# The spectral middle of a GFNet block on the 64-row halves of the matmul array

## The chip, the cores and the metric

The kernel runs on one core of one Trainium2 chip. The core has a matmul engine (PE, with its weight loads listed as PEld), three elementwise engines (DVE, ACT, POOL) and DMA queues, which are fed here by SP and by POOL. The metric is the device time of one execution in microseconds (us); lower is better.

## What is computed

A pre-norm transformer block on 2048 tokens of width 576 in bfloat16: a two-dimensional Fourier filter as the mixer, and a GeGLU feed-forward network.

```python
def _A_ref(x, w_r, w_i):
    B, S, D = x.shape
    X = rfft2(x.astype(float32), axes=(-2, -1))
    X = X * (w_r + 1j * w_i)                  # w: [2048, 289]
    return irfft2(X, s=(S, D), axes=(-2, -1)).astype(bfloat16)

def _B_ref(x, w_gate, w_up, w_down):          # [576, 4608] twice, [4608, 576]
    return (gelu(x @ w_gate) * (x @ w_up)) @ w_down

h = x + _A_ref(layernorm(x), w_r, w_i)
h2 = h + _B_ref(layernorm(h), w_gate, w_up, w_down)
```

## The kernel before

Every instruction is written out by hand. `Prog` keeps, for each tile's key, the last writer and the readers, and turns them into semaphore waits; each engine runs its own list strictly in the order in which it was filled. PE does not wait for its own earlier matmuls, except where an operation names them (`after`). The order of the stages is written as strings of short words: `SEQ1` for stage A, `SEQF` for the spectral middle, `SEQ` for the inverse stage. A letter is a step, the number says which piece, and a table beside it (`DENG`, `BENG`, `VENG`) says which engine evicts it from PSUM.

**Stage A** (`a_mm`, L532). The 2048 tokens are 128 partitions times 16 tiles c. One matmul per tile, column block and half of D does the first part of the token transform, with tables `ATS` scaled by the layer norm's 1/sigma, into `U`. Five column blocks k: 1 and 3 are differences and need the negated second half of x (`XN[...,0:288]`, made by `x_neg`, L548, step n, on POOL), 0 and 2 are sums, 4 is the remainder of 32 + 32 columns (`x_tail`, L553, step t, on POOL, copies one of them beside the other). Tiles go through in six groups; for groups 2, 3 and 4 POOL also scales the tables (`ln1_scale`, L501, step x); M0 to M5 are the groups' matmuls. The evictions into `U` (`a_ev`, L543) are shared by ACT and DVE.

**The spectral middle** works on 16 pieces i, one residue g each (`GORD` is 1 to 15, then 0). For every piece:

- D (`st_D`, L609): the real transform over the 576 columns, 2 outputs (odd and even) of 3 matmuls each, 128x288, into a pair of PSUM banks; evicted to `CUS` (576 elements a partition).
- B (`st_B`, L619): the last part of the token transform, 4 matmuls of 128x288 with 128-row tables `BT`; evicted to `YS`.
- T (`st_T`, L628): the product with the filter on DVE, Y times (w_r, -w_i, w_i, w_r): 1152 products a partition from `YS` and `WS` into `TP`. `WS` holds three planes, the third of which DVE makes as the negated w_i (`st_w`, L633, step w).
- Z (`st_Z`, L639 and L642): DVE adds the products in pairs, the 256 main columns into `ZS`, the last 32 into `ZR`, four pieces side by side.
- V (`st_V`, L649): back over the tokens, 4 matmuls of 128x256, one PSUM bank, evicted to `V` by ACT.
- R (`st_R`, L661 and L664): the same for the 32 remaining columns of four pieces at once, 2 matmuls; DVE multiplies the result by a mask `MK` into `VR`.

**After it**: I and N (L726, L764), the inverse transform over columns and the last part over tokens, which adds to x in `XO`. Eight token tiles (`NPRE`) are done here; the other eight are put between the matmuls of the first quarter's `down` (`def_i`, `def_n`, with tiles `EB`, `QB`, `YB`, `JD`). Then the feed-forward network in four quarters of 512 tokens: `gu_part` (L848) does gate and up; since 576 is 4.5 times 128 it runs on the 64-row halves of the array, two matmuls side by side on partitions 0 to 63 and 64 to 127 with different banks, each half in a first and a second part; `down` (L935) follows.

**DMA.** SP's queue issues, one after the other: x and the A tables, FT, BT, the filter's first half (residues 0 to 8, w_i then w_r, five loads each), VT, the second half (six each), DT, IT, DP, ITD, IDT, and the up weights. POOL's queue issues the gate weights: slot 0 waits for the filter's second half, slots 1 and 2 lie where `WS` is and wait for the last T. SBUF is full, so most tiles share their place with later ones; `P.alias` passes the waits on.

Of the kernel before, what the change touches and what calls it, by code (L numbers as in the profile page):

```python
# [4 lines left out]
BF16 = mybir.dt.bfloat16  # L5
# [39 lines left out]
def build_tables():  # L45
# [26 lines left out]
    I = I.reshape(4, 16, 2, 16, 128).transpose(1, 0, 2, 3, 4)  # L72
# [63 lines left out]
    T["BTAB"] = B.reshape(2, 3, 128, 128).transpose(2, 0, 1, 3).reshape(128, -1)  # L136
    T["VTAB"] = V.reshape(2, 2, 128, 256).transpose(2, 0, 1, 3).reshape(128, -1)
# [175 lines left out]
def _build(nc, A_x, A_w_r, A_w_i, B_w_gate, B_w_up, B_w_down, out):  # L313
# [16 lines left out]
    WS = sb.alloc("WS", [128, 3, NG, K2], BF16)  # L330
    assert sb.off <= wgu_end
    sb.off = wgu_end
    V = sb.alloc("V", [128, NT, 4, NG, 8], BF16)
    VR = sb.alloc("VR", [128, NT, 2, NG, 8], BF16)
# [8 lines left out]
    sb.off = wgu_end  # L343
    EB = sb.alloc("EB", [128, 2 * HK], F32)
    QB = sb.alloc("QB", [128, 4, HK], F32)
    YB = sb.alloc("YB", [128, D], BF16)
    JD = sb.alloc("JD", [128, D], BF16)
    assert sb.off <= wgu_end + NPRE * 4 * NG * 8 * 2
# [19 lines left out]
    U = sb.alloc("U", [128, 5, NG, NT, 8], BF16)  # L368
# [8 lines left out]
    BT = sb.alloc("BT", [128, 2, 3, 128], BF16)  # L377
    VT = sb.alloc("VT", [128, 2, 2, 256], BF16)
    end1 = sb.off
    sb.off = h_off  # L380
    HT0 = sb.alloc("HT0", [128, 5, 512], BF16)

# [8 lines left out]
    YS = sb.alloc("YS", [128, 2, 2, KW], BF16)  # L391
    TP = sb.alloc("TP", [128, 2, 2, 2, KW], BF16)
    ZS = sb.alloc("ZS", [128, NZ, 2, 256], BF16)
    ZR = sb.alloc("ZR", [128, 2, 2, 128], BF16)
# [38 lines left out]
    def w_up(pl, hf):  # L433
        g0, g1 = ((0, 9), (9, 16))[hf]
        src = (A_w_r, A_w_i)[pl].tensor
        P.dma(SP, WS[0:64, 1 + pl, g0:g1, :].rearrange("p g k -> p (g k)"), bass.AP(src, g0 * K2, [[128 * K2, 16], [16 * K2, 4], [1, (g1 - g0) * K2]]),
              f"w{pl}{hf}", w=[("W", hf, pl, 0)])

    def w_down(pl, hf):
        g0, g1 = ((1, 9), (9, 16))[hf]  # L440
        src = (A_w_r, A_w_i)[pl].tensor
        for jj in range(4):
            P.dma(SP, WS[64 + jj:128:4, 1 + pl, g0:g1, :], bass.AP(src, (64 + 16 * jj + 16 - g0) * K2, [[128 * K2, 16], [-K2, g1 - g0], [1, K2]]),
                  f"w{pl}{hf}", w=[("W", hf, pl, 1 + jj)])
        if hf:
            P.dma(SP, WS[64:128, 1 + pl, 0, :], bass.AP(src, 64 * K2, [[128 * K2, 16], [16 * K2, 4], [1, K2]]), f"w{pl}{hf}", w=[("W", hf, pl, 5)])

# [8 lines left out]
    wkeys = [[("W", hf, pl, h) for pl in range(2) for h in range(5 + hf)] for hf in range(2)]  # L456
# [62 lines left out]
    def a_mm(i):  # L519
        c0, c1 = GROUPS[i]  # L520
        for k in AORD:
            b = a_bank(i, k)
            for c in range(c0, c1):
# [7 lines left out]
                for lhs, p0, p1, s, e in parts:  # L531
                    P.op(PE, lambda t, b=b, lhs=lhs, p0=p0, p1=p1, s=s, e=e, o=o, c=c: t.matmul(bank(b, p0, p1, o, o + 128), lhs, ATS[:, c, :], start=s, stop=e),  # L532
                         r=[("X", c), ("ATS", c)] + ([("XN", c)] if k % 2 or k == 4 else []) + ([("XT", c), "XZ"] if k == 4 else []), w=[("PS", b)])

    def a_ev(n, eng, late=False):
        i, k = n // 5, AORD[n % 5]
        hs = (1,) if late else (0,) if n in SPLIT else (0, 1)
        g0, g1 = 8 * hs[0], 8 * hs[-1] + 8
        c0, c1 = GROUPS[i]
        m, b, w = c1 - c0, a_bank(i, k), 128  # L540
        src = bank(b, 0, w, 0, 128 * m).rearrange("p (n g e) -> p n g e", n=m, g=16)[:, :, g0:g1, :]
# [4 lines left out]
    def x_neg(i):  # L546
        c0, c1 = GROUPS[i]
        P.op(POOL, lambda g: g.tensor_scalar(XN[:, c0:c1, 0:288], XO[:, c0:c1, 288:D], -1.0, 1.0, op0=ALU.mult, op1=ALU.mult),  # L548
             r=[("X", c) for c in range(c0, c1)], w=[("XN", c) for c in range(c0, c1)])

    def x_tail(i):
        c0, c1 = GROUPS[i]
        P.op(POOL, lambda g: g.tensor_scalar(XN[:, c0:c1, 288:320], XO[:, c0:c1, 256:288], 1.0, 1.0, op0=ALU.mult, op1=ALU.mult),  # L553
             r=[("X", c) for c in range(c0, c1)], w=[("XT", c) for c in range(c0, c1)])

    P.op(DVE, lambda v: v.memset(XN[:, :, 320:384], 0.0), w=["XZ"])
# [18 lines left out]
    P.alias([(k, c) for k in ("XN", "XT") for c in range(NT)], [("V", g, c) for g in range(NG) for c in range(2)])  # L575
# [4 lines left out]
    FB, used = {}, [0] * 8  # L580
    for t, w in enumerate(SEQF):
        k, i = w[0], w[1:].rstrip("abc")
        if k in "DB":
            late = ("V", 0) in FB or any(x[0] == "V" for x in SEQF[t:t + 4])
            b = min((0, 2, 4) if late else (0, 2, 4, 6), key=lambda b: max(used[b], used[b + 1]))
            used[b] = used[b + 1] = t + 1
        elif k in "VR":
            b = min((6, 7) if ("D", LAST) not in FB else range(8), key=lambda b: used[b])
            used[b] = t + 1
            if k == "V":  # L590
                b2 = b
                if int(i) == LAST and len(VENG[LAST]) > 1:
                    b2 = min(range(8), key=lambda b: used[b])
                    used[b2] = t + 1
                b = (b, b2)
        else:
            continue
        FB[k, int(i)] = b
# [5 lines left out]
    def st_D(i, eng=ACT):  # L604
        b0, s3 = FB["D", i], i % 3
        for o in range(2):
            b = b0 + o
            for m, us in enumerate((1 - o, 3 - o, 4) if o == 0 else (4, 1 - o, 3 - o)):
                P.op(PE, lambda t, b=b, m=m, us=us, o=o: t.matmul(bank(b, 0, 128, 0, 2 * HK), U[:, us, i, :, :], FT[:, 3 * o + (2 if us == 4 else us // 2), :], start=(m == 0), stop=(m == 2)),  # L609
                    r=[("U", q, us, i // 8) for q in range(len(GROUPS))] + ["FT"], w=[("PS", b)])  # L610
        ev(eng, CUS[:, s3, :, :].rearrange("p a (j r) -> p a j r", r=2), banks(b0, 2, 2 * HK).rearrange("p r (a j) -> p a j r", a=2),
           [("PS", b0), ("PS", b0 + 1)], [("CU", s3)])

    def st_B(i, eng=ACT):
        sl, s3, sp_ = i % 2, i % 3, 1 if GORD[i] == 0 else 0
        b0 = FB["B", i]
# [387 lines left out]
```

## Time and profile before

Three runs of the kernel took 491.55, 491.62 and 493.1 us; the median is 491.62. The profiled execution has a span of 489.7 us.

| | us | share of the span | instructions |
|---|---|---|---|
| span of the profiled execution | 489.7 | | 9878 |
| PE busy | 481.8 | 98% | 4357 |
| PEld (weight loads) | 290.9 | 59% | 4358 |
| DVE busy | 191.3 | 39% | 384 |
| ACT busy | 152.0 | 31% | 294 |
| POOL busy | 32.6 | 7% | 65 |
| L848, gate and up | 228.5 + 53.4 | 58% | 2142 + 486 |
| L935, down | 144.3 | 29% | 1152 |
| L609, D | 13.4 | 3% | 96 |
| L619, B | 9.7 | 2% | 64 |
| L628, T | 12.1 | 2% | 17 |

Shares of busy time are means over stages with different limits. PE's 98% is mostly the feed-forward network; in the spectral part DVE and ACT are full as well. The busy time of a group is the time in which at least one of its instructions ran. A mean duration is longer than the distance between two in a row, because an engine starts the next one before the last has left its pipeline. The granted clock is 1.00 in all stretches looked at.

### The profile page before, as it was taken

What the parts mean: (1) busy time and instruction counts of PE and PEld (TensorE: products, weight loads), DVE (VectorE), ACT (ScalarE), POOL (GpSimd) and SP (SyncE); (2) the same over time, 40 slices, a digit from 0 to 9 for tenths busy, and PEclk for the clock granted to TensorE, in tenths of its full rate; (3) what the DMA queues carried; (4) which work ended last, traced back from release to release, by engine and by line L of the source; (5) the groups of instructions that cost most, each with busy time, mean ns of one, the idle gap of its engine ahead of it and who ended that gap; (6) DMA issues with size and microseconds to landing.
All of it is one profiled execution on the core that took longest, in us unless ns stands there. A gap on an engine that the chain in (4) does not pass through costs nothing.

```text
span 489.7 us, 9878 instructions
## 1 busy us (share of the span) xinstructions
PE 481.8 (98%) x4357; PEld 290.9 (59%) x4358; DVE 191.3 (39%) x384; ACT 152.0 (31%) x294; POOL 32.6 (7%) x65
## 2 busy tenths in 40 slices
PE   6999999999999999999999999999999999999998
PEld 3887865555688744444577644444677544444775
DVE  7899823443455534333311144333211233333111
ACT  6999852232322223322200033233100122323000
POOL 5411541000000020000000000000000000000000
DMA  8990998111000071100000001000000000000000
GB/s 282 231 335 11 367 358 304 62 26 24 1 18 14 13 230 26 23 4 1 0 20 19 14 17 26 14 1 1 7 19 19 6 1 1 1 1 1 14 18 19
DMA packets 25147, 31.26 MB, mean 64 GB/s; under 512 B 11440, under 2 KB 17840, under 8 KB 25104
## 3 DMA queue, kind: packets, MB, share of 16 engines
q1 hardware_dynamic: 22208, 18.68, 13.4%
q0 software_dynamic: 2896, 11.95, 7.0%
q8 instruction: 34, 0.56, 0.5%
q14 instruction: 9, 0.07, 0.1%
HBM read 26.29 MB, written 2.36 MB: 58 GB/s over the span
## 4 chain that ended last, share of the span: by engine, by line
PE 93%; ACT 3%; DMA 2%; DVE 2%; SPq 1%; issue 0%; DVEq 0%
PE PS L848 57%; PE PS L935 29%; DMA XO<-in_A_x_dram 2%; PE PS L609 2%; PE PS L726 1%; DVE TP L628 1%; ACT V L601 1%; PE PS L886 1%; PE PS L764 1%; PE PS L619 1%; PE PS L532 1%; ACT U L543 1%; ACT YS L601 1%; SPq L223 1%; PE PS L900 0%
## 5 line engine op out<-in xcount | busy, mean ns | idle before, releaser
L848 PE MATMUL PS<-HT,WG 64*128 64x512 bf16 (+1 forms) x2142 | 228.5, 372 | 0.0
L848 PEld LDWEIGHTS PS<-HT,WG 64*128 64x128 bf16 x2142 | 109.4, 94 | 117.5 <-issue 0.7
L857 DVE TENSOR_TENSOR AT<-GL,PS 128x512 bf16<-128x512 bf16 x144 | 98.8, 687 | 177.5 <-ACT GL L856 177.5
L856 ACT ACTIVATE GL<-PS 128x512 bf16<-128x512 f32 x144 | 85.9, 597 | 262.1 <-PE PS L848 248.7
L935 PE MATMUL PS<-WD,AT 128*128 128x288 bf16 (+2 forms) x1152 | 144.3, 286 | 0.0
L935 PEld LDWEIGHTS PS<-WD,AT 128*128 128x128 bf16 x1152 | 110.8, 98 | 30.7 <-ACT GL L856 1.3
L938 DVE TENSOR_TENSOR OS<-PS,XO 128x288 bf16<-128x288 f32 (+2 forms) x32 | 14.6, 457 | 100.4 <-PE PS L935 100.4
L848 PE MATMUL PS<-HT,WGX 64*128 64x512 bf16 x486 | 53.4, 376 | 0.0
L848 PEld LDWEIGHTS PS<-HT,WGX 64*128 64x128 bf16 x486 | 23.7, 94 | 28.8
L755 ACT ACTIVATE JD<-XO,NM 128x576 bf16<-128x576 bf16 x8 | 6.2, 775 | 28.4 <-DVE XO L903 28.4
L609 PE MATMUL PS<-FT,U 128*128 128x288 bf16 x96 | 13.4, 286 | 0.0
L628 DVE TENSOR_TENSOR TP<-YS,WS 128x1152 bf16<-128x1152 bf16 (+2 forms) x17 | 12.1, 720 | 2.1 <-ACT YS L601 1.6
L532 PE MATMUL PS<-ATS,XO 128*128 128x128 bf16 x96 | 8.8, 219 | 3.4 <-POOL ATS L501 2.4
L475 DVE BATCH_NORM_STATS2 ST<-XO 128x6 f32<-128x288 bf16 x26 | 10.0, 442 | 2.3 <-DMA XO<-in_A_x_dram 2.2
L609 PEld LDWEIGHTS PS<-FT,U 128*128 128x128 bf16 x96 | 9.2, 98 | 2.4
L601 ACT ACTIVATE CUS<-PS 128x576 bf16<-128x576 f32 x16 | 10.2, 658 | 0.8 <-PE PS L609 0.4
L601 ACT ACTIVATE YS<-PS 128x576 bf16<-128x576 f32 x16 | 10.0, 654 | 0.7 <-DVE TP L628 0.7
L619 PE MATMUL PS<-CUS,BT 128*128 128x288 bf16 x64 | 9.7, 286 | 0.3 <-ACT CUS L601 0.3
L543 ACT ACTIVATE U<-PS 128x384 bf16<-128x384 f32 (+2 forms) x28 | 9.6, 414 | 0.9 <-PE PS L532 0.9
L532 PEld LDWEIGHTS PS<-ATS,XO 128*128 128x128 bf16 x96 | 6.8, 98 | 5.0 <-POOL ATS L501 3.0
L903 DVE TENSOR_TENSOR XO<-PS,XO 128x576 bf16<-128x576 f32 x8 | 6.1, 757 | 8.0 <-PE PS L900 8.0
L601 ACT ACTIVATE V<-PS 128x512 bf16<-128x512 f32 (+1 forms) x17 | 8.9, 588 | 0.0
(79 smaller groups left out, 206.0 us busy)
## 6 DMA issues: line engine op xcount, KB each, us to landing
WD<-in_B_w_down_dram POOLq DMA_DIRECT2D x9, 576.0 KB, 12.0
WG<-in_B_w_up_dram SPq DMA_DIRECT2D x4, 1152.0 KB, 7.7
WG<-in_B_w_gate_dram POOLq DMA_DIRECT2D x4, 1152.0 KB, 10.1
out_dram<-OS SPq DMA_DIRECT2D x30, 72.0 KB, 1.6
XO<-in_A_x_dram SPq DMA_DIRECT2D x3, 576.0 KB, 7.2
WGX<-in_B_w_up_dram SPq DMA_DIRECT2D x1, 1152.0 KB, 5.9
WGX<-in_B_w_gate_dram POOLq DMA_DIRECT2D x1, 1152.0 KB, 9.7
HT<-HN SPq DMA_TRANSPOSE x60, 2.4
```

The source lines that it names most:

```text
L475: P.op(DVE, lambda v: v.bn_stats(ST1[:, c, h, :], XO[:, c, 288 * h:288 * h + 288]), r=[("X", c)], w=[("ST1", c, h)])
L532: P.op(PE, lambda t, b=b, lhs=lhs, p0=p0, p1=p1, s=s, e=e, o=o, c=c: t.matmul(bank(b, p0, p1, o, o + 128), lhs, ATS[:, c, :], start=s, sto ...
L543: fn = (lambda v: v.tensor_copy(dst, src)) if eng == DVE else (lambda a: a.activation(dst, src, ACTF.Copy))
L601: fn = (lambda v: v.tensor_copy(dst, src)) if eng == DVE else (lambda a: a.activation(dst, src, ACTF.Copy))
L609: P.op(PE, lambda t, b=b, m=m, us=us, o=o: t.matmul(bank(b, 0, 128, 0, 2 * HK), U[:, us, i, :, :], FT[:, 3 * o + (2 if us == 4 else us // ...
L619: P.op(PE, lambda t, b=b, tb=tb, m=m, s3=s3, sp_=sp_: t.matmul(bank(b, 0, 128, 0, KW), BT[:, sp_, tb, :], CUS[:, s3, m, :], start=(m == 0) ...
L628: P.op(DVE, lambda v: v.tensor_tensor(TP[:, sl, :, :, q0:q1], y4, w4, op=ALU.mult), r=[("Y", sl), ("Wn", i)] + (wkeys[0] if 1 <= g < 9 els ...
L848: op = P.op(PE, lambda t, h0=h0, kt=kt, wt=wt, b=b, s=(not second and j == 0), e=(second and j == n - 1): t.matmul(bank(b, 0, 128, c0, c1) ...
L856: P.op(ACT, lambda a: a.activation(GL[:, s2, :], bank(b0), ACTF.Gelu_apprx_tanh), r=[("PS", b0)], w=[("GL", s2)])
L857: P.op(DVE, lambda v: v.tensor_tensor(AT[:, f, :], GL[:, s2, :], bank(b0 + 1), op=ALU.mult), r=[("GL", s2), ("PS", b0 + 1)], w=[("AT", f)])
L935: P.op(PE, lambda t, b=b, d0=d0, d1=d1, f=f, p=p: t.matmul(bank(b, 0, 128, 0, d1 - d0), AT[:, f, 128 * p:128 * p + 128], WD[:, f, d0:d1], ...
L938: P.op(DVE, lambda v, b=b, d0=d0, d1=d1, p=p, c=c: v.tensor_tensor(OS[:, p % 2, d0:d1], bank(b, 0, 128, 0, d1 - d0), XO[:, c, d0:d1], op=A ...
```

## The change

The middle is rebuilt so that D, B, V and R run on the two 64-row halves of the array.

- **Order of rows.** The 128 rows are sorted into two halves jp of 64, of which each holds 32 frequency rows and the 32 mirrored ones. U has 32 groups of 4 (`[128, 5, 2*NG, NT, 4]`), V is `[128, 2, 2, NT, 2, NG, 4]`; the tables are made for it.
- **D** has a first part (step D: per half three matmuls, tail included) and a second (step d: per half two), on halves h, each half writing the other output bank in the second part. The d remainder tail is held twice, side by side, once for each half: `x_tail` writes 64 columns at two places, and the memset of the padding goes; `x_neg` covers 256 columns a tile instead of 288.
- **B**: 4 matmuls on 64 rows, one table pair per half.
- **The filter is kept twice**, once on the partitions of its own half and once on the other's: `WS` is `[128, 2, 2, NG, K2]`. Each load by SP is cut in more pieces. Copies are made by `dup_w`: residues 1 to 5 by POOL (w_i) and DVE (w_r, step w), the others by DMAs on POOL's queue, from SBUF to SBUF. The gate weights' slot 0 follows them on that queue and no longer has a wait of its own.
- **T** is two DVE instructions, 1024 products into `TP` (five buffers) and 128 into `TR`. The negated plane, the additions Z and the step z are gone: PE adds the products while it accumulates V and R.
- **V**: steps V and v, 8 matmuls of 64x128 each, two banks. **R**: steps R and r, 4 each; for q < 3 ACT copies the result to `RB` and POOL multiplies by the mask, in two instructions; for q = 3, 4 DVE does it.
- The strings and engine tables are new; some evictions of CUS, YS and V go to DVE. PSUM banks are handed out in pairs.
- `EB`, `QB`, `YB`, `JD` move from V's place to that of `HT0`.

```diff
-        P.op(POOL, lambda g: g.tensor_scalar(XN[:, c0:c1, 288:320], XO[:, c0:c1, 256:288], 1.0, 1.0, op0=ALU.mult, op1=ALU.mult),
-             r=[("X", c) for c in range(c0, c1)], w=[("XT", c) for c in range(c0, c1)])
-
-    P.op(DVE, lambda v: v.memset(XN[:, :, 320:384], 0.0), w=["XZ"])
+        x3 = XO[:, c0:c1, :].rearrange("p c (a b) -> p c a b", a=2)[:, :, :, 256:288]
+        for h in range(2):
+            o3 = XN[:, c0:c1, 256 + 64 * h:320 + 64 * h].rearrange("p c (a d) -> p c a d", a=2)
+            P.op(POOL, lambda g, o3=o3: g.tensor_scalar(o3, x3, 1.0, 1.0, op0=ALU.mult, op1=ALU.mult),
+                 r=[("X", c) for c in range(c0, c1)], w=[("XT", c, h) for c in range(c0, c1)])
...
+    def halves(key, second, plans, mm):
+        seqs = plans[::-1] if second else plans
+        prev = turn_over.get(key, [None, None])
+        for j in range(len(seqs[0])):
+            for h in range(2):
+                o = h ^ second
+                op = mm(h, o, seqs[h][j], not second and j == 0, second and j == len(seqs[0]) - 1, [prev[o]] if second and j == 0 else [])
+                turn_over.setdefault(key, [None, None])[o] = op
...
+        def mm(h, o, us, first, last, after):
+            return P.op(PE, lambda t: t.matmul(bank(b0 + o, 0, 128, 0, 2 * HK), U[64 * h:64 * h + 64, us, 2 * i:2 * i + 2, :, :], FT[64 * h:64 * h + 64, 3 * o + (2 if us == 4 else us // 2), :],
+                                               start=first, stop=last), r=[("U", q, us, i // 8) for q in range(len(GROUPS))] + ["FT"], w=[("PS", b0 + o)], after=after)
...
+        for m in range(2):
+            for h in range(2):
+                P.op(PE, lambda t, m=m, h=h: t.matmul(bank(b0 + h, 0, 128, 0, KW), BT[64 * h:64 * h + 64, sp_, m, :], CUS[64 * h:64 * h + 64, s3, m, :], start=(m == 0), stop=(m == 1)),
+                     r=[("CU", s3), "BT"], w=[("PS", b0 + h)])
...
+    def st_T(i, hs=(0, 1)):
+        g, sl, z = GORD[i], i % NY, i % NZ
+        q, j = (i // 4 % 2, i % 4) if i < LAST else (0, 0)
+        for h in hs:
+            q0, q1 = ((0, 256), (256, KW))[h]
+            w3 = WS[:, 0, 0, g, 1 + q0:1 + q1]
+            w4 = bass.AP(w3.tensor, w3.offset, [list(w3.ap[0]), [2 * NG * K2, 2], [NG * K2, 2], [1, q1 - q0]])
+            y4 = YS[:, sl, :, q0:q1].unsqueeze(2).to_broadcast([128, 2, 2, q1 - q0])
+            dst = TR[:, q, :, :, 32 * j:32 * j + 32] if h else TP[:, z, :, :, :]
+            P.op(DVE, lambda v, dst=dst, y4=y4, w4=w4: v.tensor_tensor(dst, y4, w4, op=ALU.mult),
...
+            return P.op(PE, lambda t: t.matmul(bank(b0 + o, 0, 128, 128 * c, 128 * c + 128), TP[64 * h:64 * h + 64, z, o, t_, c:256:2], VT[64 * h:64 * h + 64, 0 if g else 1 + o, t_, :],
+                                               start=first, stop=last), r=[("T", z), "VT"], w=[("PS", b0 + o)], after=after)
...
+        eng = POOL if q < 3 else DVE
+        if eng == POOL:
+            ev(ACT, RB[:, q % 2, :, :], banks(b0, 2, 128), [("PS", b0), ("PS", b0 + 1)], [("RB", q % 2)])
...
+    def dup_w(k, jp, pl=slice(0, 2), eng=None):
+        a, b = 64 * jp, 64 - 64 * jp
+        n = ("Wd", k, jp, pl.start)
+        for g0, g1 in (((1, 6),), ((6, 9),), ((9, 13),), ((13, 16), (0, 1)))[k]:
+            dst, src = (WS[q:q + 64, jp, pl, g0:g1, :].rearrange("p a g k -> p a (g k)") for q in (b, a))
...
+            if eng is None:
+                P.dma(POOL, dst, src, f"wd{k}{jp}", r=r, w=[(*n, g0)] + [("Wd", 0, jp, q, 1) for q in range(2) if g0 == 0])
+            elif eng == DVE:
+                P.op(DVE, lambda v: v.tensor_copy(dst, src), r=r, w=[(*n, g0)])
+            else:
+                P.op(POOL, lambda v: v.tensor_scalar(dst, src, 1.0, 1.0, op0=ALU.mult, op1=ALU.mult), r=r, w=[(*n, g0)])
+    for jp in range(2):
+        dup_w(0, jp, slice(1, 2), POOL)
+    for k in range(1, 4):
+        for jp in range(2):
+            dup_w(k, jp)
+    wg_load(0, 0)
```

The new order of the middle begins and ends so:

```python
SEQF = """D0 D1 w1 d0 D2 d1 d2 w0 B0 D3 B1 d3 B2 D4 d4 T0 T1 D5 B3 d5 D6 T2 B4 T3 D7 d6 d7 V2 V1 v2 v1 V0 B6 v0 D8 T4 B5 T5 ...
 ... B15 V10 T13 B14 v10 V12 R2 v12 r2 T14 V11 T15 V13 v11 V14 v13 v14 R3 V15 r3 v15 R4 r4""".split()
```

More of the change, by code (lines that the diff above doesn't have):

```diff
@@ L578, in _build @@
     LAST = NG - 1
-    FB, used = {}, [0] * 8
+    FB, used, busy = {}, {0: -8, 2: -7, 4: -6, 6: -5}, set()
     for t, w in enumerate(SEQF):
         k, i = w[0], w[1:].rstrip("abc")
[L583 to L598, printed above, removed]
+        if k in "DBVR":
+            b = min((b for b in used if b not in busy), key=lambda b: used[b])
+            FB[k, int(i)] = b
+            used[b] = t
+            if k in "DVR":
+                busy.add(b)
+        elif k in "dvr":
+            b = FB[k.upper(), int(i)]
+            used[b] = t
+            busy.discard(b)
     def ev(eng, dst, src, r, w):
@@ L602, in ev @@
         P.op(eng, fn, r=r, w=w)
[L604 to L612, printed above, removed]
```

259 lines of the change are left out of this document (138 added, 121 removed).

## The prediction

> **What bounds it now.** I read the table by stretches of time first, for where the spectral middle lies; then the chain of work that ended last, for what releases the stage behind it; then the groups with shapes apart, for the price of one instruction; then timelines, for the spacing of instructions in a full queue (a duration contains a tail that the next one overlaps). The middle runs from 19.57, the first D matmul, to 48.38, the first of L726. The columns are PE, PEld, DVE, ACT and POOL busy, then clock, DMA share, GB/s:
>
> ```profile
> 19.50:23.30 3.80, 3.80 (x36) 2.92 (x34) 2.18 (x9) 3.18 (x8) 0.00 (x0) 1.00 1.14 221
> 23.30:33.00 9.70, 9.70 (x83) 7.78 (x81) 9.60 (x23) 9.47 (x17) 1.52 (x2) 1.00 1.06 351
> 33.00:42.00 9.00, 9.00 (x78) 7.30 (x78) 8.58 (x21) 8.31 (x16) 0.00 (x0) 1.00 0.37 111
> 42.00:48.40 6.40, 5.83 (x50) 4.42 (x49) 6.28 (x17) 6.40 (x14) 1.12 (x2) 1.00 0.09 6
> ```
> Three engines are full at once, POOL is nearly empty, and the DMA engines are full until about 33. The chain of waits shows the hand-over (start, us, what):
>
> ```profile
> 45.50 2.74 ACT V L601 x6
> 48.24 0.14 issue
> 48.38 1.63 PE PS L726 x12
> ```
> So PE waits for the last evictions by ACT; six in a row cost 0.46 us each. Before 42 the same chain lies on DVE, in TP, ZS and ZR. The groups (count, busy, mean ns):
>
> ```profile
> L609 PE MATMUL PS<-FT,U 128*128 128x288 bf16 x96 | 13.4, 286 | 0.0
> L628 DVE TENSOR_TENSOR TP<-YS,WS 128x1152 bf16<-128x1152 bf16 x15 | 11.3, 756 | 2.1 <-ACT YS L601 1.6
> L619 PE MATMUL PS<-CUS,BT 128*128 128x288 bf16 x64 | 9.7, 286 | 0.3 <-ACT CUS L601 0.3
> L649 PE MATMUL PS<-VT,ZS 128*128 128x256 bf16 x64 | 8.6, 273 | 0.1
> L639 DVE TENSOR_TENSOR ZS<-TP 128x512 bf16<-128x512 bf16 x16 | 6.7, 418 | 0.1
> ```
> In a row they come closer: the chain has six of L609 in 0.73 us (0.122 each), L649 follows every 0.109. PE: (96+64) x 0.122 + (64 of L649 + 10 of L661) x 0.109 = 27.6 of 28.8 us. Anything that shortens only one engine would gain little.
>
> **PE, part by part.** D becomes 160 matmuls on 64 rows, B 64, V 256 and R 40, the last two with 128 columns. The price of two halves side by side is in the later stage, the price of a 128-column matmul in the transposes (a timeline piece, and a piece of the chain):
>
> ```profile
> 60.00 0.40 PE L848 MATMUL PS<-HT,WG 64*128 64x256 bf16 x4
> 57.91 0.58 PE PS L813 x10
> ```
> One L848 of 256 columns takes 0.269, so the fourth starts 0.13 after the first: a pair every 0.11, its second half 0.02 after its first. A pair thus costs what one full-height matmul costs (L649: 0.109). So D and B: 224 x 0.061 = 13.7; V and R: a pair per 0.058 or a little less (0.056), so 296 x 0.028 = 8.3. Sum 22.0 against 27.6: 5.6 less. No row has pairs of 128 columns. Bounds: 0.020 a half (the spacing inside a pair), 5.9; or 0.058 a half, no overlap, 17.2. I take 0.028, nearest to the L848 pair, which overlaps fully. The second half of each D, V and R also waits for PE's own earlier matmul in the other half (37 waits). That matmul takes 0.22 to 0.29; between lie mostly 4 to 8 others, 0.22 to 0.36. Bounds 0 and 37 x 0.1 = 3.7.
>
> **DVE.** ZS, ZR and the sign flips (L633) go; the product T of 1024 + 128 elements stays as two instructions. The old T15 was cut so, and shows the price (start, us):
>
> ```profile
> 46.16 0.82 DVE L628 TENSOR_TENSOR TP<-YS,WS 128x1024 bf16<-128x1024 bf16 x2
> 46.90 0.42 DVE L639 TENSOR_TENSOR ZS<-TP 128x512 bf16<-128x512 bf16 x1
> 52.56 0.76 DVE L601 CAST GS<-PS 128x576 bf16<-128x576 f32 x1
> ```
> 0.74 for both, 16 x 0.74 = 11.8. Evictions come over from ACT: after T0 five of 576 elements (CUS, YS) at 0.67 (the cast above to the next start, 53.23) = 3.4; V once whole and eight halves, by the 192-element casts of L543 (0.265 apart, so 0.33 for 256, 0.60 for 512) = 3.2; four mask products on 384 and 128 elements, between L664's 256 (0.42) and 768 (0.96), less the 0.07 that overlap = 1.4. Sum 19.9 after T0; before it was 23.5 in 25.0 us. ACT falls from 24.8 to 25 x 0.54 + 7 x 0.46 + 11 x 0.28 = 19.8 and is no bound.
>
> **What is added in front.** The tail copies (x_tail) on POOL become two of double size a group. POOL is full there:
>
> ```profile
> 16.50 0.27 POOL L553 TENSOR_SCALAR XN<-XO 128x96 bf16<-128x96 bf16 x1
> 16.86 0.91 POOL L548 TENSOR_SCALAR XN<-XO 128x864 bf16<-128x864 bf16 x1
> 12.63 0.23 PE L532 MATMUL PS<-ATS,XO 128*128 128x128 bf16 x1 [1.97 <-POOL ATS L501]
> ```
> 96 elements 0.27 and 864 0.91 make 0.19 + 0.00083 an element; 192 then cost 0.35, and each instruction 0.08 more to the next. A group of three gains 2 x 0.43 - 0.35 = 0.51, one of two 0.44, x_neg loses 0.08. From t2 at 7.78 on: four x 0.51 + 0.44 - three x 0.08 = 2.2, of which 0.5 fits into POOL's wait before n3. So n5 ends at 17.77 + 1.7, and the last matmul group M5, whose second matmul reads it at 18.12, moves by 1.4. Bounds 0 (if POOL had hidden slack) and 2.2. D starts at 21.0, not 19.57.
>
> Then T0. DVE's last U cast ends at 21.2 + 1.4 = 22.6; in its queue follow two copies of the filter (64x1445; L633's 1156 took 0.45), CUS of D2 and YS of B1 (0.67 each): T0 at 24.9, before 23.27. POOL's two copies, 1445 elements at 1.4 each, start when its NM work is done (19.5 + 1.7) and end at 24.1: hidden by that DVE queue; if that cover is gone, T0 slips by what they are late. SP issues six more filter loads, at 0.6 each; DT, IT and the rest queue behind and come up to 3.8 later than 30, with I needing them at 46. The other copies are six DMA pieces or more on POOL's queue, ahead of the gate load, which is not needed before 56. T5 reads the first at about 24.9 + 5 x 0.74 + 0.67 + 0.60 + 0.67 = 30.6; issued at 24.1, 0.4 MB, I take 30 for the landing (bounds: 27, and 34.2 by the gate load's 10.1 us from issue to landing).
>
> **POOL against DVE.** POOL takes the mask products of R0 to R2, six of 512 elements; L501's 384 cost 0.83, so about 1.05 each. DVE does feel POOL: of the seven scalings in L506 one took 467 ns, and it started at 17.35 inside POOL's 16.86 to 17.77.
>
> ```profile
> L506 DVE TENSOR_SCALAR ATS<-ATB,RS x7: 241/249/467, 6.7 to 17.9; 128x128 bf16<-128x128 bf16 x7
> ```
> One collision cost 0.22; L793 has one of 0.15. Six x 0.19 = 1.1; bounds 0 and 6 x 1.05 = 6.3. The Trainium skill (SBUF — State Buffer, section Who interferes with whom) says that a DVE instruction with two SBUF inputs, as T is, contends with a GpSimd one that reads SBUF, and that whoever comes second waits for the whole of the first. The row agrees (the scaling ended as POOL's did). By that rule alone up to 6.3 would be lost instead of 1.1.
>
> **What I cost at nothing.** V, U and the tables keep their number of instructions behind the middle (48 of L726). EB, QB, YB and JD move into HT0: their first writer, def_i, then waits for the last gate/up matmul of the first 512 tokens, which PE has issued just before; without that cover def_n, 22 matmuls later (22 x 0.122 = 2.7 us), would wait.
>
> **The sum**, on DVE: 24.9 + 19.9 + 1.0 of idle (before 1.5; ACT feeds it sooner now; bounds 0 and 1.5) + 1.1 = 46.9; the last two mask products (0.45) need not be done when I starts: 46.45. PE alone: 21.0 + 22.0 + up to 3.7 = 43.0 to 46.7, no later. Against 48.38 this is 1.9 less; from I on all is as before. The profiled execution, 489.7, becomes 487.8; the median of the runs is 1.9 above its span, so **489.7** (491.62 - 1.9).
>
> **Rivals.** (1) More is gained: no collisions, no idle, x_tail half hidden. DVE would end at 24.2 + 19.9 - 0.45 = 43.7, PE at 20.3 + 22.0 + half its own waits, 1.9, = 44.2: 4.2 less, 487.4. For it: the last stretch before was ACT's, which is relieved. Against: three engines never ran without gaps. Chance 0.18.
> (2) The hand-overs eat it: PE's own waits at 0.1 and DVE's at 1.5 come one after the other instead of beside each other; end 48.2, 491.4. For it: 37 new waits in PE's only queue, with everything of D, B and V behind each. Chance 0.16.
> (3) Slower: the copies for T5 land late. Price by the gate load, 10.1 us: 34.2 against 30.6, so 3.6 on every T behind it: 493.3. It decides from a landing after 32.5. For it: the DMA share is 1.06 in that stretch. Against: 0.4 MB is a third of the gate load. Chance 0.15.
> (4) Slower: POOL's mask products stop DVE for their full length, 5.2 more than in the sum: 494.9. Chance 0.08; the two collisions seen were partial.
> (5) Halves of 128 columns do not overlap: PE 22.0 + 8.9, from 21.0 with before's gaps of 1.2 to 53.1: 4.7 over, 496.3. Chance 0.05. This is also what the Trainium skill (TensorE: Matmul & The Clock Gate, section LDWEIGHTS) would lead one to: a load costs by its columns, whatever its rows, so halves double the loads. But the pairs of L848 start 0.02 apart with a load each.
>
> **Numbers.** The forecast has 0.38, with 488.6 to 490.9 as its own range. A change under 0.3% (1.5 us) can't be told from none; a quarter of the forecast's chance (0.10) and 0.10 of (2) lie there: same 0.20. Faster: 0.28 + 0.18 + 0.05 of (2) = 0.51. Slower: (3), (4), (5) and the last 0.01 of (2), 0.29. The range goes to the better end of (1) and into (4): 486.6 to 494.9.
>
> **What would show it.** D starts near 21.0 and T0 near 24.9; L690 pairs every 0.056; DVE without ZS, T in 0.74; L782 starting near 46.5. Wrong if the first D is at 19.6, if T5 waits for a DMA, if T grows beside POOL's mask products, or if PE idles for its own semaphore over 4 us in all.

## The result, and the profile after

The changed kernel took 512.95 us (median of four runs, 512.3 to 513.69) beside 491.59 (491.38 to 493.1) for the kernel before on the same chip: a ratio of 1.0425, interval 1.0406 to 1.0445. The profiled execution has a span of 511.3 us where before it was 489.7. The 21.6 us between the spans lie ahead of the inverse stage: its first matmul (L782 now, L726 before) starts at 69.96 instead of 48.38, 21.58 later; from there to the first gate/up matmul it is 11.19 us in both.

The table by stretches of time, changed kernel (PE, PEld, DVE, ACT and POOL busy, then granted clock, DMA share, GB/s):

```profile
19.50:25.10 5.60, 5.43 (x79) 3.73 (x76) 2.90 (x11) 3.96 (x11) 4.87 (x10) 1.00 0.59 141
25.10:42.50 17.40, 0.03 (x2) 0.03 (x4) 1.25 (x3) 0.65 (x1) 5.32 (x9) 0.58 1.01 259
42.50:56.00 13.50, 13.43 (x228) 9.38 (x230) 11.05 (x25) 10.02 (x19) 0.39 (x1) 0.78 0.31 105
56.00:70.00 14.00, 11.12 (x251) 8.01 (x247) 14.00 (x28) 9.91 (x21) 9.10 (x9) 1.00 0.05 11
```

For 17.4 us PE stands still, and DVE for 18.4; POOL's 5.32 us are its issuing of DMAs, and only the DMA engines are full (1.01). Behind that PE is full first, at a clock of 0.78, and then DVE, without a gap. DVE's timeline shows who waits (start, us, what, in brackets the idle time ahead of it and what ended that):

```profile
41.22 0.53 DVE L731 COPY WS<-WS 64x1445 bf16<-64x1445 bf16 x1 [18.38 <-DMA WS<-WS]
41.67 0.74 DVE L616 CAST CUS<-PS 128x576 bf16<-128x576 f32 x1
42.45 0.53 DVE L731 COPY WS<-WS 64x1445 bf16<-64x1445 bf16 x1
43.01 0.76 DVE L616 CAST YS<-PS 128x576 bf16<-128x576 f32 x1
43.68 0.68 DVE L682 TENSOR_TENSOR TP<-YS,WS 128x1024 bf16<-128x1024 bf16 x1
```

The first of DVE's two filter copies stands for 18.38 us, and it waits for a copy made by DMA, though it reads nothing that a copy DMA writes. D2's eviction is behind it in DVE's queue, B1's too, and so PE's bank and T0. The chain of waits says which DMA it is:

```profile
24.48 2.89 DMA WS<-in_A_w_r_dram
27.37 0.28 issue
27.65 1.19 POOL WS L239 x2
28.89 1.77 POOL WS L239 x3
30.66 10.53 DMA WS<-WS
41.22 0.53 DVE WS L731
...
53.28 0.73 PE PS L690 x24
...
68.68 1.14 DVE VR L717 x3
69.96 1.63 PE PS L782 x12
```

It is the last one of POOL's queue, issued at 30.66 and landed 10.53 us later: the copy of residue 0. In `dup_w` this DMA also takes the keys of the engines' copies as written, `("Wd", 0, jp, q, 1)`. A row has 289 elements of 2 bytes, so the last element of residue 0 and the first of residue 1 share a word of 4 bytes, and the program puts the two writes in an order (no run leaves the order out, so that it is needed is not shown). It does so by emission: POOL's copies are emitted ahead of the DMAs, and the DMAs follow them; DVE's come out of `SEQF` (w1, w0), behind the DMAs, and therefore wait for the last of them.

The groups that answer to those of before (count, busy, mean ns, idle ahead):

```profile
L649 PE MATMUL PS<-FT,U 64*128 64x288 bf16 x160 | 16.1, 319 | 0.2 <-DVE U L563 0.2
L690 PE MATMUL PS<-VT,TP 64*128 64x128 bf16 x256 | 10.5, 217 | 1.6 <-DVE CUS L616 1.0
L682 DVE TENSOR_TENSOR TP<-YS,WS 128x1024 bf16<-128x1024 bf16 x16 | 12.0, 751 | 0.7 <-ACT YS L616 0.6
L717 POOL TENSOR_TENSOR VR<-RB,MK 128x512 bf16<-128x512 bf16 x6 | 7.8, 1300 | 24.2 <-ACT RB L616 24.0
```

A row of V matmuls in the chain, 24 in 0.73 us, gives 0.030 each. TP's mean of 751 ns hides two kinds: 684 ns alone, and up to 1320 beside POOL's masks, which take 1300 on average. One meeting, in the timeline of all engines:

```profile
65.20 1.15 POOL L717 TENSOR_TENSOR VR<-RB,MK 128x512 bf16<-128x512 bf16 x1 [1.38 <-ACT RB L616]
65.37 1.06 DVE L682 TENSOR_TENSOR TR<-YS,WS 128x128 bf16<-128x128 bf16 x1
```

TR starts 0.17 after the mask and ends 0.08 after it (66.43 against 66.35); alone it takes 0.22. So it stood until the mask was nearly through. Three TR and two TP do this, and lose 2.5 and 1.1 us. It also goes the other way round: where a TP had started at 60.98, the mask that came 0.02 later (61.00) took 1.70 instead of 1.04. That is the rule of the Trainium skill (SBUF — State Buffer, section Who interferes with whom) that the second waits for the whole of the first; the trace agrees.

### The profile page after: what moved, and what is told of

It reads as the page before. It is cut to its first block, busy times and chain, and to the rows that moved or that the text cites. A ratio compares the mean times of both kernels' runs of the same rounds, so it can differ in the third digit from the quotient of the medians.

```text
span 511.3 us, 10453 instructions
## 1 busy us (share of the span) xinstructions
PE 483.2 (95%) x4644; PEld 289.6 (57%) x4644; DVE 192.5 (38%) x378; ACT 147.8 (29%) x288; POOL 50.2 (10%) x87
## 4 chain that ended last, share of the span: by engine, by line
PE 88%; SPq 4%; DVE 3%; DMA 3%; POOL 1%; issue 0%; DVEq 0%
PE PS L904 55%; PE PS L990 28%; SPq L239 4%; DMA WS<-WS 2%; PE PS L649 1%; DVE TP L682 1%; PE PS L782 1%; PE PS L941 1%; PE PS L820 1%; DVE TR L682 1%; POOL WS L239 1%; DMA WS<-in_A_w_r_dram 1%; PE PS L690 0%; DVE V L616 0%; PE PS L669 0%
## 5 line engine op out<-in xcount | busy, mean ns | idle before, releaser
L669 PE MATMUL PS<-CUS,BT 64*128 64x288 bf16 x64 | 7.5, 313 | 17.4 <-DVE CUS L616 17.4
L649 PE MATMUL PS<-FT,U 64*128 64x288 bf16 x160 | 16.1, 319 | 0.2 <-DVE U L563 0.2
L616 ACT ACTIVATE YS<-PS 128x576 bf16<-128x576 f32 x13 | 8.4, 652 | 19.0 <-PE PS L669 17.9
L669 PEld LDWEIGHTS PS<-CUS,BT 64*128 64x128 bf16 x64 | 3.0, 101 | 18.8 <-DVE CUS L616 17.7
L552 PE MATMUL PS<-ATS,XO 128*128 128x128 bf16 x96 | 9.9, 242 | 3.2 <-POOL ATS L521 2.1
L682 DVE TENSOR_TENSOR TP<-YS,WS 128x1024 bf16<-128x1024 bf16 x16 | 12.0, 751 | 0.7 <-ACT YS L616 0.6
L690 PE MATMUL PS<-VT,TP 64*128 64x128 bf16 x256 | 10.5, 217 | 1.6 <-DVE CUS L616 1.0
L552 PEld LDWEIGHTS PS<-ATS,XO 128*128 128x128 bf16 x96 | 7.9, 110 | 4.5 <-POOL ATS L521 2.6
L649 PEld LDWEIGHTS PS<-FT,U 64*128 64x128 bf16 x160 | 7.7, 105 | 4.7 <-PE PS L649 0.6
L717 POOL TENSOR_TENSOR VR<-RB,MK 128x512 bf16<-128x512 bf16 x6 | 7.8, 1300 | 24.2 <-ACT RB L616 24.0
```

Of the source, the lines that this page charges most:

```text
L649: return P.op(PE, lambda t: t.matmul(bank(b0 + o, 0, 128, 0, 2 * HK), U[64 * h:64 * h + 64, us, 2 * i:2 * i + 2, :, :], FT[64 * h:64 * h + ...
L669: P.op(PE, lambda t, m=m, h=h: t.matmul(bank(b0 + h, 0, 128, 0, KW), BT[64 * h:64 * h + 64, sp_, m, :], CUS[64 * h:64 * h + 64, s3, m, :], ...
L682: P.op(DVE, lambda v, dst=dst, y4=y4, w4=w4: v.tensor_tensor(dst, y4, w4, op=ALU.mult), r=[("Y", sl), *dup[(i >= 5) + (i >= 8) + (i >= 12) ...
L690: return P.op(PE, lambda t: t.matmul(bank(b0 + o, 0, 128, 128 * c, 128 * c + 128), TP[64 * h:64 * h + 64, z, o, t_, c:256:2], VT[64 * h:64 ...
```

## The experiments

Where a kernel's stages begin, in the profiled execution of each (us): the first D matmul, T0, the first matmul of the inverse stage, and the stretch between the last two. The ratio is to the kernel before, from runs beside it.

| kernel | D | T0 | I | T0 to I | median | ratio and interval |
|---|---|---|---|---|---|---|
| before | 19.57 | 23.27 | 48.38 | 25.11 | 491.59 | |
| changed | 21.20 | 43.68 | 69.96 | 26.28 | 512.95 | 1.0425 (1.0406 to 1.0445) |
| e1 | 21.36 | 43.15 | 69.29 | 26.14 | 511.69 | 1.0399 (1.0379 to 1.0419) |
| e2 | 21.80 | 42.61 | 69.40 | 26.79 | 511.83 | 1.0405 (1.0386 to 1.0424) |
| e3 | 21.30 | 25.00 | 50.11 | 25.11 | 493.48 | 1.0036 (1.0024 to 1.0048) |
| e4 | 22.26 | 46.19 | 70.06 | 23.87 | 514.59 | 1.0458 (1.0412 to 1.0505) |
| e5 | 21.54 | 26.94 | 53.36 | 26.42 | 496.66 | 1.0122 (1.0079 to 1.0165) |
| e6 | 21.91 | 27.30 | 51.53 | 24.23 | 494.07 | 1.0050 (1.0035 to 1.0065) |
| e7 | 22.47 | 27.88 | 52.41 | 24.53 | 495.50 | 1.0073 (1.0055 to 1.0090) |
| e8 | 19.95 | 24.75 | 48.62 | 23.87 | 491.83 | 1.0008 (0.9996 to 1.0020) |
| e9 | 20.04 | 24.69 | 52.97 | 28.28 | 498.69 | 1.0149 (1.0127 to 1.0171) |
| e10 | 20.07 | 24.72 | 54.56 | 29.84 | 498.06 | 1.0130 (1.0102 to 1.0159) |
| e11 | 20.25 | 25.04 | 48.38 | 23.34 | 491.11 | 0.9990 (0.9977 to 1.0004) |
| e12 | 19.87 | 24.67 | 47.45 | 22.78 | 491.22 | 1.0003 (0.9990 to 1.0016) |

D differs by over 1 us between kernels that are equal up to there (21.20 to 22.47), so a step of less than that between two single profiles is not read as an effect.

A part of this spread has a cause that the traces show, the granted clock in stage A. The stretch from 14 to 18, in the changed kernel, in e1 and in e7:

```profile
14.00:18.00 4.00, 4.00 (x46) 3.92 (x44) 3.01 (x15) 3.40 (x11) 3.25 (x7) 0.57 1.11 239
```

```profile
14.00:18.00 4.00, 2.99 (x52) 2.68 (x49) 3.52 (x15) 3.88 (x12) 3.25 (x7) 1.00 1.11 216
```

```profile
14.00:18.00 4.00, 4.00 (x46) 4.00 (x47) 2.13 (x11) 2.52 (x8) 2.62 (x5) 0.62 1.10 212
```

In each of the three PE has waited 2.1 us for POOL's tables just before; in the first and the third the clock then fell to 0.50, in e1 it stayed up. In e4, e6 and e7 it fell earliest, before 14, and there the traces show how it reaches D: ACT waits for PE twice, 0.70 to 0.75 us each time, its 1/sigma comes late, DVE waits for that (1.87 us in e7), and POOL's last table scaling waits 0.80 to 0.83 us for DVE. D starts at 21.91 to 22.47. In the changed kernel and e3, where the clock fell later, and in e1, POOL has no such wait, and D starts at 21.20 to 21.36. So the second tail copy alone moves D to about 21.3, and the slow clock can add up to 1.1 to that. No profile without that copy (before, e8 to e12) has a clock under 1.00 in this stretch. Why e1's stayed up is open.

**e1: DVE's copies emitted ahead of the last DMAs.**

```diff
-    for k in range(1, 4):
+    for k in range(1, 3):
...
-    wg_load(0, 0)
...
         if w[0] == "w":
             dup_w(0, i, slice(0, 1), DVE)
+            if i == 0:
+                for jp in range(2):
+                    dup_w(3, jp)
+                wg_load(0, 0)
```

> The changed kernel with one thing moved: the four copy DMAs of the last group (residues 13 to 15 and 0) and the gate load of slot 0 are put into POOL's queue after DVE's two copies, so that they wait for DVE and DVE no longer waits for them. Theory S (in the changed kernel DVE's first copy waits for the last copy DMA, 18.4 us): T0 goes back to about 25 and the middle ends some 17 to 21 us earlier. By my forecast's sum alone 489.7. With what the changed kernel's trace adds to that sum, 495: the copies for residue 9 landed at 37.9 there, and T8's turn would be at 34.5 (3.4 more), and T beside POOL's mask products took 3.6 us more than alone, of which the sum had 1.1 (2.5 more). Rival (the stall only hid another limit, the loads themselves or POOL's queue): over 503.

Measured: 511.69, only 1.26 us below the changed kernel. DVE's timeline:

```profile
23.05 1.73 DVE L731 COPY WS<-WS 64x1445 bf16<-64x1445 bf16 x1
...
25.47 0.66 DVE L731 COPY WS<-WS 64x1445 bf16<-64x1445 bf16 x1
26.15 0.76 DVE L616 CAST YS<-PS 128x576 bf16<-128x576 f32 x1
43.15 0.69 DVE L682 TENSOR_TENSOR TP<-YS,WS 128x1024 bf16<-128x1024 bf16 x1 [16.24 <-issue]
```

The copies now run at 23.05 and 25.47, and T0 waits in their place. T0 reads the key of the copied rows, the last to write that key is now the DMA of residue 0, and its semaphore is full at 43.07. The wait had moved from a write behind a write to a read behind a write. A second thing shows: the first copy takes 1.73 us beside POOL's copies (21.50 to 24.38), where it took 0.53 in the changed kernel with POOL idle.

**e2: e1 with all masks on DVE.**

```diff
-        eng = POOL if q < 3 else DVE
+        eng = DVE
```

> As the first, and the mask products of R0 to R2 go from POOL (with ACT's copy to RB) to DVE, straight from PSUM: six of 512 elements. Theory P (POOL stops DVE's T for most of its instruction): T returns to 0.74 everywhere, which gives 3.6 us back, and the six products cost DVE 6 x 0.6 = 3.6: within 1 us of the first run. Rival (the port costs what the forecast had, 1.1): 2.5 slower than the first run.

Measured: 511.83 against e1's 511.69, the same. The long products are gone (no TR over 0.23 us, no TP over 0.7), and three such lines have come in DVE's timeline, 3.9 us together:

```profile
59.33 1.29 DVE L717 TENSOR_TENSOR VR<-PS,MK 128x512 bf16<-128x512 f32 x2 [0.26 <-PE PS L706]
```

Price and saving are equal within 0.7 us (T0 to I): the 3.6 us are POOL's masks in DVE's way, and the work itself costs DVE as much.

**e3: the kernel before, with a second tail copy on POOL** that writes the zeros that were there already.

```diff
+        x3 = XO[:, c0:c1, :].rearrange("p c (a b) -> p c a b", a=2)[:, :, :, 256:288]
+        o3 = XN[:, c0:c1, 320:384].rearrange("p c (a d) -> p c a d", a=2)
+        P.op(POOL, lambda g: g.tensor_scalar(o3, x3, 0.0, 1.0, op0=ALU.mult, op1=ALU.mult),
...
```

> The kernel before, with a second tail copy of the same size a group on POOL; it writes zeros where the memset wrote them, so nothing else changes. It has two instructions of 96 or 64 elements instead of two of 192 or 128, and x_neg keeps 288 columns. Theory (POOL's queue sets the end of stage A): per group of three 0.35 more, of two 0.32; from t2 on 4 x 0.35 + 0.32 = 1.7, less 0.5 of slack = 1.2 later for M5: 492.8. Rival (POOL has slack there): 491.6, no difference.

Measured: 493.48, 1.9 us more than before (expected were 1.2). D starts 1.73 later, T0 and I also 1.73 later: stage A's loss goes through the middle unchanged.

**e4: the changed kernel with 138 spare matmuls ahead of B2**, so that PE isn't idle in the stall.

```diff
     def st_B(i, eng=ACT):
+        if i == 2:
+            for _ in range(138):
+                P.op(PE, lambda t: t.matmul(bank(6, 0, 128, 0, 2 * HK), FT[:, 0, 0:128], FT[:, 0, :], start=True, stop=True), r=["FT"], w=[("PS", 6)])
```

> The changed kernel with its stall, and 138 matmuls of 128x288 into a free bank on PE ahead of B2, where PE otherwise idles for 17.4 us; the results are not read. Theory C (the granted clock of 0.50 in the first 6 us after the stall is part of the loss): PE works at full clock from 42.5 on, D, B and V up to 48.7 take half: 3 us less, 510. Rival (DVE and its T set the pace after the stall): within 0.7 of 513.

Measured: 514.59 (511.96 to 517.0), no gain in the time. Its stretches say more than that:

```profile
25.10:42.50 17.40, 17.40 (x152) 13.61 (x147) 0.00 (x0) 1.53 (x3) 6.35 (x11) 1.00 0.97 227
42.50:56.00 13.50, 11.54 (x232) 8.29 (x229) 12.02 (x27) 9.69 (x19) 0.28 (x1) 1.00 0.46 152
```

With the clock at 1.00 PE is no longer full behind the stall (11.54 of 13.5, in the changed kernel 13.43), and T0 to I takes 23.87 instead of 26.28. But in this execution the last copy landed at 43.70 instead of 41.19, so I starts at the same time. That the cold clock costs some 2.4 us behind the stall is what these two profiles show; the time doesn't confirm it, and why the copy landed later is open. In e6, where PE does not stand still ahead of T0, T0 to I is 24.23, which agrees.

**e5: the order of e1, but the DMA follows the copies.** The keys go from what the DMA writes to what it reads; T0 depends on the engines' copies alone.

```diff
-                P.dma(POOL, dst, src, f"wd{k}{jp}", r=r, w=[(*n, g0)] + [("Wd", 0, jp, q, 1) for q in range(2) if g0 == 0])
+                P.dma(POOL, dst, src, f"wd{k}{jp}", r=r + [("Wd", 0, jp, q, 1) for q in range(2) if g0 == 0], w=[(*n, g0)])
```

> Edit: as in e1_copies_reordered, VectorE's two filter copies are emitted ahead of the last pair of copy DMAs, and these DMAs now read the keys of the copied rows of the first residues instead of writing them: the DMA waits for the copies (at their shared word of 4 bytes), and the first product no longer waits for the DMA. Theory 'one ordering': in e1 the first product waited 16.2 us for nothing but the landing of the last copy DMA (43.07). Without that it starts near 27 (VectorE's copies ended at 26.1 in e1), the rest of the middle keeps its 27 us, and the time is 511.7 - 16.2 = 495.5 us (493.5 to 498), still above 491.6, the rest being stage A (1.4 to 1.9) and the products beside POOL's masks (3.6). Rival 'late transfers': the stall only moves on to the products that truly need the copied rows (the sixth, ninth and thirteenth, rows landed at 30, 38 and 43 in e1): then the trace shows VectorE idle before these, and with only 10 us left of the stall regained the time is 500 or more.

Measured: 496.66, 15.0 us below e1: one ordering of two writes was the stall. T0 starts at 26.94. What is left of rival 'late transfers' shows in DVE's timeline, at T8 and T12:

```profile
37.84 1.32 DVE L682 TENSOR_TENSOR TP<-YS,WS 128x1024 bf16<-128x1024 bf16 x1 [0.81 <-issue]
...
43.43 0.69 DVE L682 TENSOR_TENSOR TP<-YS,WS 128x1024 bf16<-128x1024 bf16 x1 [1.99 <-DMA WS<-WS]
```

Their rows landed at 37.76 and 43.35; 2.8 us go to these two waits.

**e6: e5 with SP's later loads held until the last copy has landed.**

```diff
+                after_wd3 = [("Wd", 3, jp, 0, g) for jp in range(2) for g in (13, 0)]
+                P.dma(SP, IT[:, :, :, :].rearrange("p a b c -> p (a b c)"), dram["ITAB"][:, :], "it", r=after_wd3, w=["IT"])
...
+                wg_load(0, 0, after_wd3)
```

> Edit: e5_copies_ordered, and SyncE's loads of the inverse tables (IT, DP, ITD, IDT) and of the up half of slot 0 wait for the last copy DMA, so that from 25 us on the copies share the DMA engines only with DT and the gate load. Theory 'one ordering': the products come no earlier than their rows anyway, and the time is that of e5 within 1 us, unless the held loads come too late for their readers. Rival 'late transfers': the copies land at 33 to 36 in place of 43, VectorE's idle time before the sixth to thirteenth product goes, and the time falls by 2 to 6 us against e5.

Measured: 494.07, 2.6 less than e5, in rival 'late transfers'' range, though the copies land later than it expected: the last at 39.12 (in e5 at 43.35). Only one product waits, the sixth (T5), 0.52 us for rows that landed at 33.56. From T0 to I it is 24.23. The lines from DVE's timeline that set T0 (line numbers of this and the later kernels differ somewhat):

```profile
23.59 1.66 DVE L727 COPY WS<-WS 64x1445 bf16<-64x1445 bf16 x1
...
25.94 0.65 DVE L727 COPY WS<-WS 64x1445 bf16<-64x1445 bf16 x1
...
27.30 0.68 DVE L678 TENSOR_TENSOR TP<-YS,WS 128x1024 bf16<-128x1024 bf16 x1
```

**e7: e6 with all masks on DVE** (the edit of e2).

> Edit: e6_other_loads_held with all five pairs of masks on VectorE out of the PSUM bank, none on POOL, no copy into RB. Port theory: the products beside POOL's masks took 3.6 us more in the changed kernel; six products of 0.55 us on VectorE (3.3 us) take their place, so the time is that of e6 within 1 us. Rival (the products' longer times come from something else, such as the DMA traffic): the 3.3 us come on top, 3 us slower than e6, with the long TP and TR rows still there.

Measured: 495.5, 1.4 more than e6, between the two expectations. The long products are gone again, as the port theory has it. T0 to I is 0.3 longer and D 0.56 later in the profiles; so at most a small part is the masks' price, and the rest lies in stage A, where the two kernels are equal.

**e8: e6 without any tail copy.** The remainder's matmul is split into four of 32 columns, each with its own strip of partitions, and reads `XO` directly; the twelve copies on POOL go.

```diff
-                    parts = [(XN[:, c, 256:384], 0, 128, True, True)]
+                    parts = [(XO[:, c, d0:d0 + 32], 32 * q, 32 * q + 32, True, True) for q, d0 in enumerate((256, 544) * 2)]
...
```

> Edit: e6_other_loads_held, and in stage A the remainder chunk (k = 4) reads its columns straight out of XO: four matmuls of 32 columns each (256 to 287 and 544 to 575, twice) into partitions 0, 32, 64 and 96 of the bank, in place of one matmul of 128 columns out of XN; POOL's twelve tail copies (8 of 0.350 and 4 of 0.298 us, 4.0 us together) are left away. Theory 'POOL's tail copies pace stage A': the middle starts 1.5 to 2 us earlier and the time is 492.3 us (491.5 to 493). Rival 'PE paces': 48 more matmuls lie in the stage's full PE stretches (14 to 21 us); at 0.06 us each they cost 2.9 us, and the time is 495 or more.

Measured: 491.83, 2.2 less than e6 and the time of the kernel before. (This and the later runs were on another chip, where the kernel before took 491.71 to 491.72; by the ratios it is 2.1.) D starts at 19.95. PE doesn't mind the 48 matmuls more. The remainder of a group of three tiles, in PE's timeline:

```profile
16.95 0.22 PE L548 MATMUL PS<-ATS,XO 128*128 128x128 bf16 x1
17.01 0.22 PE L548 MATMUL PS<-ATS,XN 128*128 128x128 bf16 x1
17.16 0.35 PE L548 MATMUL PS<-ATS,XO 128*32 128x128 bf16 x12
```

All twelve start within 0.13 us (0.35 less the 0.22 that one takes), as three matmuls of full width at their spacing of 0.06 would: the four strips of a tile run side by side. Only the change to strips costs more, 0.15 ahead of the first. POOL now ends its two filter copies at 22.04, and DVE's take 0.81 and 0.53 instead of 1.66 and 0.65.

**e9: the copy DMAs on SP's queue**, the first pair ahead of the second W half's last loads, the engines' copies cut to residues 1 to 3.

```diff
-        for g0, g1 in (((1, 6),), ((6, 9),), ((9, 13),), ((13, 16), (0, 1)))[k]:
+        for g0, g1 in (((1, 4),), ((4, 9),), ((9, 13),), ((13, 16), (0, 1)))[k]:
...
-                P.dma(POOL, dst, src, f"wd{k}{jp}", r=r + [("Wd", 0, jp, q, 1) for q in range(2) if g0 == 0], w=[(*n, g0)])
+                P.dma(SP, dst, src, f"wd{k}{jp}", r=r + [("Wd", 0, jp, q, 1) for q in range(2) if g0 == 0], w=[(*n, g0)])
...
```

> Edit: e8_no_tail_copies, with all copy DMAs issued by SyncE ahead of DT, IT and the rest (the first pair ahead of the last W half), none by POOL, and the engines' copies cut to residues 1 to 3 (VectorE and POOL 0.6 of their length each), the first pair of DMAs taking 4 to 8. Theory 'start of the products': in e6 the first product starts at 27.30, after two VectorE copies of 1.66 and 0.65 us, the first beside POOL's own copies; here POOL's end before VectorE's begin, each takes 0.4 to 0.5, and the first product starts 1.4 to 2 us earlier against the stage's end; the time falls by 1.5 to 2.5 us against e8. Rival 'rows': the copied rows still decide, VectorE shows idle time before the fourth, ninth or thirteenth product, and the time is that of e8 or above.

Measured: 498.69, 6.9 more than e8. T0 isn't earlier (24.69 against 24.75; e8 had already taken most of the gain), the fourth product (T3) waits 0.55 for its rows, and T8 longer:

```profile
39.41 0.69 DVE L695 TENSOR_TENSOR TP<-YS,WS 128x1024 bf16<-128x1024 bf16 x1 [4.00 <-issue]
```

The edit did one thing that was not meant: the gate load, with no copies ahead of it in POOL's queue, was issued at 21.14 (e8: 32.36), and the second W half, issued until 29.23, landed at 34.04 (e8: 28.53). So the gate load's place is the likely cause; no run moves it alone. Whether SP's queue would serve the copies better otherwise isn't answered.

**e10: e9 with D7's and D13's casts on ACT.**

```diff
-DENG, BENG = ['act', 'act', 'dve', 'act', 'act', 'act', 'act', 'dve', 'act', 'act', 'act', 'act', 'act', 'dve', 'dve', 'act'],
+DENG, BENG = ['act', 'act', 'dve', 'act', 'act', 'act', 'act', 'act', 'act', 'act', 'act', 'act', 'act', 'act', 'dve', 'act'],
```

> Edit: e9_sync_queue_copies, and the CUS casts of D7 and D13 go from VectorE to ScalarE. Theory 'VectorE paces the middle' (busy 30.6 of 32 us in e6 from 20 to 52, ScalarE 24.4): two casts of 0.74 us leave the pacing engine, the time falls by 1.0 to 1.5 us against e9. Rival 'hand-overs': ScalarE is as late as VectorE where it matters; no change within 0.5 us, or slower.

Measured: 498.06; the intervals of e9 and e10 overlap. With the rows late (in its profile T3 waits 5.39 us, for a copy that landed at 32.33), DVE isn't what paces here, so this says nothing on the question.

**e11: e8 with the V casts of V8, V9 and V10 whole on ACT; e12: D13's cast there too.**

```diff
-... ('act', 'dve'), ('act', 'dve'), ('act', 'dve'), ('act',), ('act',), ('act', 'dve'), ('act', 'dve'), ('act',)]
+... ('act',), ('act',), ('act',), ('act',), ('act',), ('act', 'dve'), ('act', 'dve'), ('act',)]
```

> Edit: e8_no_tail_copies, and the V casts of residues V8, V9 and V10, split between ScalarE and VectorE so far (0.39 and 0.41 us), go to ScalarE whole (0.60 us). Theory 'VectorE paces the middle' (in e8 it is busy 27.1 of the 28 us from 20 to 48, without a gap from 36 on; ScalarE has 2.1 us idle from 36 to 44): 3 x 0.41 = 1.2 us leave VectorE, the time falls by 0.8 to 1.2 us, to 490.6 to 491.0. Rival 'hand-overs' (a longer cast on ScalarE holds its pair of banks and so TensorE and the next casts): no change within 0.4 us, or slower.

> Edit: e11_late_v_on_act, and D13's CUS cast (0.74 us on VectorE) goes to ScalarE (0.65 us). Theory 'VectorE paces the middle': 0.7 us less than e11, about 490.1 us, 1.5 us below the kernel before. Rival 'hand-overs': the time of e11 or above, because ScalarE, with 0.63 + 0.65 us more from 36 to 44 against 2.1 us idle there, is late with the casts that the products wait for.

Measured: 491.11 and 491.22 beside 491.71 for the kernel before. Neither interval leaves out 1, so no version was found that can be told from the kernel before, and e11 and e12 can't be told from each other. In the profile of e12 the middle is shorter, as the theory has it: T0 to I 22.78 against e8's 23.87 (1.1, expected 1.9). The middle's row, e8's and then e12's:

```profile
24.70:48.60 23.90, 21.03 (x462) 15.44 (x459) 23.50 (x51) 19.34 (x39) 12.66 (x14) 1.00 0.85 250
```

```profile
24.70:47.50 22.80, 20.86 (x463) 15.29 (x459) 21.98 (x47) 20.04 (x40) 11.96 (x14) 1.00 0.86 257
```

DVE falls by 1.52 us and ACT rises by 0.70; DVE is still the fullest engine.

## Why the prediction was wrong

It said 489.7 and I at 46.45; measured were 512.95 and 69.96. The 23.5 us between are 18.8 ahead of T0 (43.68 for 24.9) and 4.7 behind it (26.28 from T0 to I for 21.55).

- **The step that failed** is the one behind stage A: DVE's last U cast, then "in its queue follow two copies of the filter", at 0.45 each. What a queue holds next was taken as what runs next; the semaphore in front of the copy was not priced. It stood 18.38 us. The diff has the reason, the keys of k = 0 in the list of writes of a DMA that is emitted ahead of the copy. e5 shows the cause: its T0 is at 26.94, 16.7 earlier, and the time 16.3 below the changed kernel's.
- **The same step, smaller:** the copies were priced by an instruction that ran alone. Beside POOL's copies, which I had noted as ending at 24.1 and called hidden, the first takes 1.66 us, and the second, just behind them, 0.65 (e6): 2.31 for both, not 0.90. In the changed kernel itself they ran after the stall, at 0.53.
- **Late copies (rival 3)** were put at the sixth product, T5, with a landing at 30. That pair landed at 29.66, and at 30.43 in e5, where T5 did not wait; only in e6, where it landed at 33.56, did T5 wait, for 0.52 us. T8 and T12, which read the later pairs, have no term in the sum. Theirs landed at 37.92 and 41.19 in the changed kernel, hidden by the stall; with the stall gone they cost 2.6 us (e5 against e6).
- **POOL against DVE (term 1.1, rival 4 6.3):** 3.6 us in the changed kernel, 3.3 to 3.7 in e6 and e8. The rule of rival 4 was right, each meeting costs until the first is through; but five products meet a mask badly, not six for their full length. The 0.19 was too small: the scaling that was shown had started at 17.35, in the second half of POOL's 16.86 to 17.77, and waited for the rest only.
- **Stage A:** D at 21.0 forecast, 21.20 measured; e3 gets 1.9 from one extra tail copy alone, e8 takes the loss away. This step held, with POOL as its cause; that the clock would fall in stage A (0.57 from 14 to 18) was not foreseen.
- **PE:** 0.028 a half forecast, 0.030 measured for 24 in a row; rival 5, the halves that do not overlap, did not come. But the 5.6 us that PE saves are nowhere in the time: in e8 it is busy 21.03 of 23.9 us, and DVE 23.50.
- **T0 to I** at 21.55: without stall, late rows and tail copies (e8) it is 23.87, and 2.2 of the 2.3 us over are the port's (3.3 for 1.1). The changed kernel's 26.28 has some 2.4 more, which e4's profile puts to the cold clock. Against the kernel before, e8's T0 is 1.5 later, and the stretch behind it is 1.2 shorter where 3.5 were forecast: without the stall, too, the mis-sized port term would have eaten the forecast gain of 1.9.

So the 21.4 us of the result are, in the order in which they were taken away: the ordering 16.3 (changed to e5), transfers that share the DMA engines 2.6 (e5 to e6), the tail copies 2.2 (e6 to e8, of which some 0.6 may be the clock in e6's stage A), and 0.2 that can't be told from nothing. Without these three the new middle takes the old one's time.

## What to carry to other kernels

An instruction's place in its queue is not its start: read the wait in front of every instruction that a change adds, and ask which of its semaphores rises last. Where a program puts two writers in an order, the order has to be chosen on purpose, the slow one behind the fast one; and the slow one must not stand as the last writer of a key that an early reader needs. And a change that relieves an engine which isn't alone at the limit gives the time to the next one, here DVE, whose own work it cut least.

## What the runs showed of the hardware

- A copy of 289 KB from SBUF to SBUF over POOL's queue took 9.7 us to land in the changed kernel (issued 28.24, landed 37.92), with a DMA share of 1.01 from 25.1 to 42.5, and 5.5 in e8 (29.41 to 34.95), with SP's loads held and a DMA share of 0.91.
- After 17.4 us without matmuls the granted clock was 0.50, and it stayed there for some 6 us of full PE work: 0.50 still from 46 to 48, 0.88 from 48 to 50, 1.00 from 50. In stage A it also fell after a wait of 2.1 us (0.57 from 14 to 18 in the changed kernel), but not in every profile (1.00 in e1 after the same wait).
- Four matmuls of 32 columns into four strips of a bank, with 128 moving columns, run side by side: twelve start within 0.13 us (e8). So columns that do not lie side by side can be read where they are; copying them together first had cost 2.2 us of the whole.
